# A gated recurrence and a maxout feed-forward on one core: 64x64 update tiles, a compact fp32 state, one PSUM ring and another written order

## The chip, the cores and the metric

The kernel runs on one core of a Trainium2 chip. TensorE (PE) multiplies matrices from SBUF into PSUM; VectorE (DVE), ScalarE (ACT) and GpSimd (POOL) work on elements, each an in-order queue with its own semaphores; SyncE (SP) issues nearly all DMAs, in order, to 16 DMA engines. [...] The metric is device time in microseconds (us) from the first to the last instruction and what lies around it; smaller is better.

## The reference, cut to what matters

```python
batch, n_heads, seq, head_dim = (4, 8, 768, 48)      # q, k, v, alpha: fp32
for t in range(S):
    state = alpha[:, :, t, :, None] * state + einsum('bhd,bhe->bhde', k[:, :, t], v[:, :, t])
    y[:, :, t] = einsum('bhd,bhde->bhe', q[:, :, t], state)
x = y.transpose(0, 2, 1, 3).reshape(B * S, H * D)    # 3072 x 384
h = maximum(maximum(x @ w1, x @ w2), x @ w3)         # w: 384 x 768
out = h @ w_out                                      # 768 x 384, fp32
```

Each of 8 heads keeps a 48 x 48 state that decays by alpha, row by row, and takes the outer product of k and v at every token.

## The kernel before, in words

**Steps.** The 3072 tokens are twelve steps of 256 tokens (`s`; batch `s % 4`, the part of the sequence `s // 4`). A step is two chunks of 128 tokens (`x` = 0, 1), which are worked on together: partitions 0 to 63 hold the first chunk, 64 to 127 the second, and each partition holds two neighbouring tokens (`r` = 0, 1). Steps s and s+4 belong to the same batch, so the state passes from chunk 0 to chunk 1 of a step, and from chunk 1 to chunk 0 of step s+4.

**One step, piece by piece.** Every piece has a letter, and the work's order is a written list of such letters. `l` loads alpha, k, q, v (384 KB each, `l0`, `l2` for q, and so on, L95), into rings of four. `m` multiplies the alphas of a token pair (L184), `N` takes the logarithm (L188), `r` makes 1/alpha (L193, L195), `u` and `w` shift k and q of the first token by it (L199, L203). `c` sums the logarithms on TensorE (L209, L212), `e`, `f`, `g` are the exponentials of the sums and totals on ScalarE (L217, L223, L229), `k` and `q` scale the inputs with them into fp16 (L235), `V` scales v (L156, L158). `T` turns scaled k and q with eight TensorE transposes a half (L259) and `t` copies them out of PSUM; from step 6 on `D` has a DMA do this instead (L267). `A` makes the scores (L280) and `a` masks them (L287). `Y` makes the output of both chunks (L311 from the state, L330 from the masked scores and v), `x` copies it to fp16 (`xT`).

**The state.** `S` makes the products of k and v of a chunk (L368). Two heads share 128 columns, so a product is 128 x 96 and only its two diagonal blocks of 48 are wanted. `s` adds the old state from the fp16 tile `st` into `full`, fp32 128 x 384 (L379). `M` makes the decay `gm` from the totals in two small operations (L353, L355); its second factor `half_c` is zero for the unwanted block of each partition. `z` multiplies `full` by `gm` into the other `st` (L383): this clears the unwanted blocks, and `Y` reads `st` directly.

**Feed-forward.** `G` makes one of nine gate products of a step (L396, six matmuls of 256 columns; three column blocks times w1, w2, w3). `h` copies the first of three on ScalarE (L150) and takes the maximum with the other two on VectorE (L411). `O` multiplies by w_out for one chunk (L420, six matmuls of 384 columns), `o` scales into `ob` and stores it (L428). `K` loads a weight block and `W` casts it. `H` issues matmuls on a tile of zeros that nobody reads (L433): fillers.

**Order.** There is no scheduler: each engine executes its instructions in the order in which the pieces are emitted. PROLOGUE is a free list for the first steps, STEADY is repeated for each step from the fourth on, and LAST ends it. A piece is a letter, an index, the engine if not the usual one (v VectorE, p GpSimd, a ScalarE), and the step after `@`. PSUM banks come from three rings, by a tag: `"w": 2, "s": 2, "g": 4` (work, state and output, gate). A piece that needs a bank takes one that is free at that place of the list, and its first matmul waits for whoever read the bank last.

**The output stage around the change.** Each chunk's output is three blocks of 128 columns (`f`) in one bank, made in four strips of 32 PSUM partitions (`m`). The state part goes in tiles of 128 rows by 32 columns, the chunk part in tiles of 64 by 32, and its order is

```python
        from_state(0, True)
        from_chunk((0, False), (1, True))
        from_state(1, False)
        from_state(2, True)
        from_chunk((2, False),)
```

Of the kernel before, what the change touches and what calls it, by code (L numbers as in the profile page):

```python
# [17 lines left out]
LAM = 0.09  # L18
# [5 lines left out]
def kernel(  # L24
# [43 lines left out]
    for u in range(U):  # L68
# [5 lines left out]
    undo = np.exp(-LAM * P)  # L74
    c32_np = np.stack(
        [np.exp(at_pair + SIGMA), np.exp(-at_token - SIGMA), undo * (rr < 64), undo * (rr >= 64)], 1
# [35 lines left out]
    c32 = cpool.tile([P, 4], FP32, name="c32")  # L112
# [5 lines left out]
    for item in """  # L118
        a0 c k0 q0 v0
    """.split():  # L120
        if item[0] == "c":
            load_const()
        elif item[0] == "w":
            load_weight(int(item[1:]))
        else:
            load(item[0], int(item[1:]))
# [3 lines left out]
    vs_c, ys_c, half_c = c32[:, 0:1], c32[:, 1:2], c32[:, 2:4]  # L130
# [29 lines left out]
    def cast_weight(_, i, eng):  # L160
# [8 lines left out]
     lps_of, dec_of, tps_of, aps_of, sps_of, gps_of, ops_of, full_of) = ({} for _ in range(19))  # L169

    banks = {"w": 2, "s": 2, "g": 4}

    def bank(shape, name, tag, dtype=FP32):
        return ps.tile(shape, dtype, name=name, tag=tag, bufs=banks[tag])
# [30 lines left out]
    def sums(s, _, tag):  # L205
        lps = bank([P, 512], "lps", tag or "w")
# [20 lines left out]
    def totals(s, *_):  # L227
        gate_of[s] = work.tile([P, HP, U, 2], FP32, name="ge", tag="ge", bufs=8)
        nc.scalar.activation(  # L229
            out=gate_of[s].rearrange("p a u b -> p (a u b)"),  # L230
            in_=lps_of[s][:, H * D:H * D + 2 * U * HP], func=AFT.Exp)
# [23 lines left out]
    def turn(s, r, tag):  # L255
        tps = bank([P, 2, HP, P], "tps", tag or "w", FP16)
# [14 lines left out]
    def scores(s, u, tag):  # L271
        aps = [bank([P, HP, P], f"aps{i}", tag or "w") for i in range(2)]
# [18 lines left out]
    def attend(s, _, tag):  # L291
# [3 lines left out]
        yps = [bank([P, NF, P], "yps", tag or "s") for _ in range(U)]  # L295
# [10 lines left out]
        def from_state(g, first):  # L306
            for x in range(U):
                for m in range(P // C) if old[x] else ():
# [4 lines left out]
                                     qkT[:, :, 0, p, x * J:(x + 1) * J], start=first, stop=not first)  # L313

        def from_chunk(*groups):
            jobs = []
            for m in range(P // C):
                todo = []
                for g, first in groups:
                    f = turns[m][g]  # L320
                    p, part = blocks[P // C * f + m]
                    cols = [(0, C * part)] * (part < 2) + [(1, D + C * (part - 1))] * (part > 0)
                    todo += [(f, first, n == 0, n == R * len(cols) - 1, i, p, n % R, at)
                             for n, (i, at) in enumerate(j for j in cols for _ in range(R))]
                jobs.append(todo)
            for n in range(max(len(j) for j in jobs)):
                for m, job in enumerate(jobs):
                    for x in range(U) if n < len(job) else ():
                        (f, first, begin, end, i, p, r, at), rows = job[n], slice(x * J, (x + 1) * J)
                        nc.tensor.matmul(  # L330
                            yps[x][C * m:C * (m + 1), f, :],
                            vt[rows, r * HP + p].rearrange("p a b -> p (a b)")[:, at:at + C],
                            lats[p // (HP // R)][rows, i, p % (HP // R) * R + r, :],
                            start=begin and (first or not old[x]),
                            stop=end and (not first or not old[x]))

        from_state(0, True)
        from_chunk((0, False), (1, True))
        from_state(1, False)
        from_state(2, True)  # L340
        from_chunk((2, False),)

# [197 lines left out]
```

## Time and profile before

| | us |
|---|---|
| median of 3 timed runs (159.69 to 161.0) | 160.05 |
| profiled execution, first to last instruction (its span; what lies around it is not in the page) | 157.2 |
| TensorE busy (2557 matmuls, 57 of them fillers) | 149.3 |
| VectorE busy (237 instructions) | 134.8 |
| ScalarE busy | 71.7 |
| GpSimd busy | 84.0 |
| gate products, 648 matmuls of mean 273 ns | 77.9 |
| output projections, 144 matmuls of mean 326 ns | 25.4 |

A matmul's duration in the page runs from its start to its modelled end, and matmuls are pipelined: gate products start 109 ns apart, and the 273 ns is not their price. Where the text counts TensorE's work, it takes the distance between starts. In the same way a VectorE instruction's row is about 0.08 us longer than the distance from its start to the next one's. Lists by group give `line engine operation output<-inputs sizes xcount | busy us, mean ns | idle time of the engine just before them <- what ended it`. Lists in order of time give start and length in us, with the idle time before a piece in brackets. The granted TensorE clock is full in all of the span, 0.9 or more in every fortieth.

### The profile page before, as it was taken

To read this page: it belongs to the slowest core of one execution; us is meant where nothing else is said; L and a number is where in the kernel's file an instruction comes from. 1 tells how busy PE (TensorE), PEld (TensorE's weight loads), DVE (VectorE), ACT (ScalarE), POOL (GpSimd) and SP (SyncE) were. 2 spreads that over 40 slices of the span, in tenths; PEclk is the share of its full clock that TensorE was granted. 3 is DMA by queue.
4 is the path that set the end of the run, shared out by engine and by line. 5 is a ranking of instruction groups with operands and counts; after the bars stand their busy time and mean duration, and the time that the engine had idled before them with its cause. 6 is when DMAs were issued, how large, how long until landed. Compare 5 with 4: busy or idle time off the path is not lost.

```text
span 157.2 us, 5971 instructions
## 1 busy us (share of the span) xinstructions
PE 149.3 (95%) x2557; PEld 111.0 (71%) x2557; DVE 134.8 (86%) x237; ACT 71.7 (46%) x146; POOL 84.0 (53%) x109
## 2 busy tenths in 40 slices
PE   6999986999999999999999999999999999999990
PEld 2346554888776796797787787877877877868850
DVE  2248999999977999999999999999999999696851
ACT  3348891776148466167165273371562621412020
POOL 5116679569325954946956928739759470100000
PEclk9999999999999999999999999999999999999999
DMA  5999999999999999369399999999709409120004
GB/s 123 321 325 325 355 355 249 329 368 261 235 291 276 301 280 321 111 168 286 68 173 274 223 252 263 136 265 202 203 5 103 134 4 203 35 80 24 4 34 167
DMA packets 70777, 31.97 MB, mean 203 GB/s; under 512 B 63328, under 2 KB 70752, under 8 KB 70752
## 3 DMA queue, kind: packets, MB, share of 16 engines
q1 hardware_dynamic: 70464, 31.46, 78.3%
q8 instruction: 20, 0.33, 0.8%
q10 hardware_dynamic: 288, 0.13, 0.6%
q14 instruction: 5, 0.04, 0.1%
HBM read 23.73 MB, written 4.72 MB: 181 GB/s over the span
## 4 chain that ended last, share of the span: by engine, by line
PE 88%; DVE 6%; ACT 2%; issue 1%
PE gps L396 44%; PE ops L420 15%; PE wps L433 9%; PE yps L330 6%; PE yps L311 4%; PE aps L280 4%; PE sps L368 3%; PE tps L259 2%; PE lps L209 1%; DVE vt L158 1%; DVE qk L235 1%; DVE hT L411 1%; DVE full L379 1%; ACT qkT L150 1%; PE lps L212 1%
## 5 line engine op out<-in xcount | busy, mean ns | idle before, releaser
L396 PE MATMUL gps<-xT,wcat 128*128 128x256 f16 x648 | 77.9, 273 | 2.3 <-DVE xT L152 2.3
L396 PEld LDWEIGHTS <-wcat 128*128 128x128 f16 x648 | 60.8, 98 | 12.4 <-ACT la L188 2.4
L287 DVE TENSOR_TENSOR lat<-aps,cp 128x512 f16<-128x512 f32 x48 | 30.5, 680 | 0.6 <-PE aps L280 0.6
L411 DVE TENSOR_TENSOR h<-gps,h 128x512 f16<-128x512 f32 x36 | 24.5, 685 | 3.1 <-PE gps L396 2.5
L411 DVE TENSOR_TENSOR hT<-gps,h 128x512 f16<-128x512 f32 x36 | 24.6, 687 | 2.4 <-PE gps L396 0.4
L420 PE MATMUL ops<-wo,hT 128*128 128x384 f16 x144 | 25.4, 326 | 0.1
L150 ACT CAST h<-gps 128x512 f16<-128x512 f32 x31 | 17.3, 584 | 13.6 <-PE gps L396 13.1
L383 POOL TENSOR_TENSOR st<-full,gm 128x384 f16<-128x384 f32 x11 | 9.3, 845 | 24.0 <-DVE full L379 20.0
L420 PEld LDWEIGHTS <-hT 128*128 128x128 f16 x144 | 14.0, 98 | 8.3 <-issue 0.3
L150 ACT CAST xT<-yps 128x384 f16<-128x384 f32 x12 | 5.8, 482 | 27.5 <-PE yps L330 27.5
L433 PE MATMUL wps<-blank 128*128 128x512 f16 x57 | 16.3, 438 | 1.2 <-DVE blank L505 1.2
L156 ACT ACTIVATE ob<-ops,c 128x384 f32<-128x384 f32 x13 | 7.3, 582 | 20.6 <-PE ops L420 20.6
L235 POOL TENSOR_TENSOR qk<-rq,ac 128x384 f16<-128x384 f32 x9 | 9.6, 1072 | 9.3 <-ACT ac L223 8.9
L203 POOL TENSOR_TENSOR qa<-rq,ra 128x384 f32<-128x384 f32 x10 | 10.0, 1001 | 4.6 <-DMA rq<-in_q_dram 4.6
L433 PEld LDWEIGHTS <-blank 128*128 128x128 f16 x57 | 6.0, 110 | 8.6 <-issue 3.7
L199 POOL TENSOR_TENSOR ka<-rk,ra 128x384 f32<-128x384 f32 x11 | 11.4, 1039 | 0.2 <-DMA rk<-in_k_dram 0.2
L235 POOL TENSOR_TENSOR qk<-rk,ic 128x384 f16<-128x384 f32 x8 | 10.2, 1274 | 1.6 <-ACT ic L217 1.6
L150 ACT COPY qkT<-tps 128x1024 f16<-128x1024 f16 x8 | 8.0, 1015 | 6.5 <-PE tps L259 6.5
L330 PE MATMUL yps<-lat,vt 64*32 64x128 f16 x768 | 10.9, 220 | 0.0
L158 DVE TENSOR_SCALAR ob<-ops,c 128x384 f32<-128x384 f32 x11 | 6.7, 608 | 3.1 <-PE ops L420 3.1
L379 DVE TENSOR_TENSOR full<-sps,st 128x384 f32<-128x384 f32 x16 | 8.8, 549 | 0.4 <-PE sps L368 0.3
L184 POOL TENSOR_TENSOR pa<-ra 128x384 f32<-128x384 f32 x9 | 9.0, 1002 | 0.0
(54 smaller groups left out, 186.7 us busy)
## 6 DMA issues: line engine op xcount, KB each, us to landing
ra<-in_alpha_dram SPq DMA_DIRECT2D x12, 384.0 KB, 4.8
rk<-in_k_dram SPq DMA_DIRECT2D x12, 384.0 KB, 5.0
rq<-in_q_dram SPq DMA_DIRECT2D x12, 384.0 KB, 5.4
rv<-in_v_dram SPq DMA_DIRECT2D x12, 384.0 KB, 5.4
out_dram<-ob SPq DMA_DIRECT2D x24, 192.0 KB, 3.5
ws<-in_moe_w_dram SPq DMA_DIRECT2D x9, 384.0 KB, 6.2
ws<-in_moe_w_out_dram SPq DMA_DIRECT2D x3, 384.0 KB, 7.6
qkT<-qk SPq DMA_TRANSPOSE x12, 4.7
```

What stands on the lines that cost most here:

```text
L150: nc.scalar.copy(out=dst, in_=src)
L199: engines[eng or "p"].tensor_mul(near_of[s, "k"], raw("k", s, 0), raw("a", s, 1))
L203: engines[eng or "p"].tensor_mul(near_of[s, "q"], raw("q", s, 0), inv1_of.pop(s))
L235: engines[eng or "p"].tensor_mul(dst.rearrange("p a b c -> p (a b) c")[:, :, :D], near_of.pop((s, n)) if r == 0 else raw(n, s, 1), dec_of[ ...
L287: nc.vector.tensor_mul(lat_of[s, u][:, i].rearrange("p (a r) t -> p a r t", r=R), aps_of[s, u][i].rearrange("p (a r) t -> p a r t", r=R), ...
L330: nc.tensor.matmul(yps[x][C * m:C * (m + 1), f, :], vt[rows, r * HP + p].rearrange("p a b -> p (a b)")[:, at:at + C], lats[p // (HP // R)] ...
L379: nc.vector.tensor_add(full, sps_of.pop((s, x)), sts[b][x].rearrange("p a (b d) -> p a b d", d=D))
L383: engines[eng or "p"].tensor_mul(sts[s % B][1 - x].rearrange("p a (b d) -> p a b d", d=D), full_of.pop((s, x)), gm_of.pop((s, x)).unsqueez ...
L396: nc.tensor.matmul(gps[:, j, :], wcat[:, f, g, jj * P:(jj + 1) * P], xT[:, f].rearrange("p u t -> p (u t)"), start=(f == 0), stop=(f == NF ...
L411: nc.vector.tensor_max(h, gps, h_of[s, i - 1])
L420: nc.tensor.matmul(ops, hT_of[s][:, jj, u * P:(u + 1) * P], wo16[:, jj, :], start=(jj == 0), stop=(jj == NJ - 1))
L433: nc.tensor.matmul(wps, blank[:, :P], blank, start=True, stop=True)
```

## The change

1. **Output stage.** All state products of a step's two chunks come first, then all chunk products, in one accumulation per bank.
2. **Update.** Each product is made in 64x64 tiles: one head's 64 (48 used) columns of k by its 48 columns of v. Only the wanted blocks are made, 320 matmuls of 48 columns for 160 of 96.
3. **State.** `full` is fp32 128 x 192. The decay `M` is one small multiplication; its constant factor moves into the bias of `g`. `z` writes `kept`, fp32 128 x 192, which the next `s` adds. A new piece `y` spreads `kept` into the fp16 `st` with zeros in the unwanted blocks, on GpSimd in one operation or on ScalarE in two.
4. **PSUM.** One ring of eight banks for all.
5. **Order.** One list for the whole run takes the place of PROLOGUE, STEADY and LAST. It begins with batches 1, 0, 3, 2; the constants are requested before the first load. Ten transposing pieces stay on TensorE (steps 0 to 4), and fourteen go by DMA (steps 5 to 11). The fillers go from 57 to 38. `V` is on ScalarE nine times (three before), `x` 16 (12), `o` 16 (13), `h` 34 (31), `y` 11. The last step's projections are in two parts each, four matmuls and two.

The core of the diff:

```diff
-        [np.exp(at_pair + SIGMA), np.exp(-at_token - SIGMA), undo * (rr < 64), undo * (rr >= 64)], 1
+        [np.exp(at_pair + SIGMA), np.exp(-at_token - SIGMA), rr < 64, rr >= 64, 0 * rr - LAM * P / 2], 1
...
-    banks = {"w": 2, "s": 2, "g": 4}
-    def bank(shape, name, tag, dtype=FP32):
-        return ps.tile(shape, dtype, name=name, tag=tag, bufs=banks[tag])
+    def bank(shape, name, dtype=FP32):
+        return ps.tile(shape, dtype, name=name, tag="bank", bufs=8)
...
-            in_=lps_of[s][:, H * D:H * D + 2 * U * HP], func=AFT.Exp)
+            in_=lps_of[s][:, H * D:H * D + 2 * U * HP], func=AFT.Exp, bias=undo_c)
...
+        for g in range(NF):
             for x in range(U):
                 for m in range(P // C) if old[x] else ():
                     f = turns[m][g]
                     p, part = blocks[P // C * f + m]
                     nc.tensor.matmul(yps[x][C * m:C * (m + 1), f, :],
                                      sts[b][x][:, p, C * part:C * (part + 1)],
+                                     qkT[:, :, 0, p, x * J:(x + 1) * J], start=(g == 0), stop=False)
...
+        for n in range(len(jobs[0])):
+            for m, job in enumerate(jobs):
+                for x in range(U):
+                    (f, begin, end, i, p, r, at), rows = job[n], slice(x * J, (x + 1) * J)
+                    nc.tensor.matmul(
+                        yps[x][C * m:C * (m + 1), f, :],
+                        vt[rows, r * HP + p].rearrange("p a b -> p (a b)")[:, at:at + C],
+                        lats[p // (HP // R)][rows, i, p % (HP // R) * R + r, :],
+                        start=begin and not old[x], stop=end and f == turns[m][-1])
...
-        gt = work.tile([P, HP], FP32, name="gt", tag="gt")
-        e.tensor_mul(gt, gate_of[s][:, :, x, 1], nxt)
-        gm = work.tile([P, HP, 2], FP32, name="gm", tag="gm", bufs=6)
-        e.tensor_mul(gm, gt.unsqueeze(2).broadcast_to([P, HP, 2]),
-                     half_c.unsqueeze(1).broadcast_to([P, HP, 2]))
+        gm = work.tile([P, HP], FP32, name="gm", tag="gm", bufs=6)
+        engines[eng or "p"].tensor_mul(gm, gate_of[s][:, :, x, 1], nxt)
...
                 for x in xs:
-                    rows = slice(x * J, (x + 1) * J)
-                    nc.tensor.matmul(sps_of[s, x][:, p],
-                                     qk[rows, r, 1, p].rearrange("p a b -> p (a b)"),
-                                     vt[rows, r * HP + p, :, :D], start=(r == 0), stop=(r == R - 1))
+                    for i in range(2):
+                        rows, cols = slice(x * J, (x + 1) * J), slice(64 * i, 64 * (i + 1))
+                        nc.tensor.matmul(sps_of[s, x][cols, p], qk[rows, r, 1, p, i],
+                                         vt[rows, r * HP + p, i, :D], start=(r == 0), stop=(r == R - 1))
...
-            nc.vector.tensor_add(full, sps_of.pop((s, x)),
-                                 sts[b][x].rearrange("p a (b d) -> p a b d", d=D))
+            nc.vector.tensor_add(full, sps_of.pop((s, x)), kept_of[b, U * c + x - 1])
...
+        kept = kept_of[b, U * c + x] = work.tile([P, HP, D], FP32, name="kept", tag="kept", bufs=6)
+        engines[eng or "p"].tensor_mul(kept, full_of.pop((s, x)),
+                                       gm_of.pop((s, x)).unsqueeze(2).broadcast_to([P, HP, D]))
+    def spread_state(s, x, eng):
+        c, b = divmod(s, B)
+        st, kept = sts[b][1 - x], kept_of[b, U * c + x]
+        if eng == "a":
+            for i in range(2):
+                nc.scalar.mul(st[:, :, D * i:D * (i + 1)], kept, half_c[:, i:i + 1])
+        else:
+            engines[eng or "p"].tensor_mul(
+                st.rearrange("p a (b d) -> p a b d", d=D), kept.unsqueeze(2).broadcast_to([P, HP, 2, D]),
+                half_c.unsqueeze(1).unsqueeze(3).broadcast_to([P, HP, 2, D]))
...
+    ORDER = """
+        l0@1 r0@1 m0v@1 N0@1 H12@0 c0@1 g0@1 f0@1 e0@1 l1@1 u0v@1 r1@1 l0@0 m0p@0 N0@0 l0@3
+        k1v@1 H10@0 c0@0 m0v@3 N0@3 H1@0 c0@3 e0@0 k0v@1 l2@1 q1v@1 l1@0 T1@1 l2@0 M0p@1 w0v@1
+        q0v@1 H1@0 T0@1 f0@0 q1p@0 r0@0 r1@0 u0v@0 t0a@1 k1v@0 l0@2 t1v@1 w0v@0 q0p@0 k0v@0 f0@3
+        g0@0 M0p@0 l3@1 g0@3 r0@2 r1@2 H5@0 A0@1 a1@1 l1@3 r0@3 a0@1 A1@1 T1@0 a3@1 H2@0 T0@0
+        t0v@0 m0p@2 V0a@1 H1@0 S0@1 u0p@3 a2@1 e0@3 k1v@3 t1a@0 k0v@3 H3@0 A0@0 s0a@1 z0p@1 N0@2
+        c0@2 a0@0 l2@3 r1@3 A1@0 a1@0 w0p@3 y0a@1 H1@0 Y0@1 l3@0 V0a@0 q0p@3 g0@2 f0@2 q1v@3
+        a2@0 S0@0 s0a@0 z0p@0 l2@2 w0p@2 q1v@2 T1@3 e0@2 l1@2 T0@3 a3@0 y0a@0 H2@0 Y0@0 x1a@1
+        x0a@1 K1@0 t0v@3 t1v@3 A0@3 A1@3 s1v@0 s1v@1 a1@3 W1a@0 k1p@2 G1@1 x0a@0 K0@0 W0a@0
...
+        q1p@9 g0@9 l3@9 h6a@7 h1v@7 A1@8 a2@8 S0@8 s0v@8 A0@8 a0@8 V0v@9 k1p@9 D1@9 k0p@9 q0p@9
+        G5@7 D0@9 r1@10 a3@8 c0@10 f0@10 g0@10 M1v@6 N0@11 l2@11 y1a@4 a1@8 O1@5 o1a@5 O0@5
+        o0a@5 h5v@7 G7@7 h7v@7 z0p@8 y0p@8 e0@10 k1p@10 u0p@10 c0@11 e0@11 h2v@7 Y0@8 f0@11
+        g0@11 x0v@8 S0@9 A1@9 A0@9 x1a@8 G6@8 M0v@9 a2@9 a1@9 l2@10 l3@10 M1p@5 z1p@5 k0p@10
+        l1@11 G3@8 h3a@8 G4@8 s0v@9 z0p@9 a0@9 y0a@9 G8@8 G7@8 h8v@7 h6a@8 M1p@7 G0@8 G5@8 a3@9
+        h7v@8 w0v@10 G1@8 h4v@8 z1p@7 y1p@5 Y0@9 q1v@10 x0v@9 M0p@10 z1v@6 x1a@9 D1@10 q0v@10
...
+        x0v@11 O0@6 o0v@6 G8@11 G0@11 h1v@10 h0a@11 O1@6 o1a@6 G6@11 G4@11 G1@11 h8v@10 h4v@10
+        h5v@10 h1v@11 h2v@10 G2@11 G7@11 G3@11 G5@11 h3a@11 h4v@11 O1@8 O0@8 o1v@8 h5v@11 o0a@8
+        O1@9 h2v@11 h6a@11 h7v@11 h8v@11 O0@9 o0v@9 o1a@9 O0@10 o0a@10 O2@11 O3@11 o0a@11 O4@11
+        O5@11 o1v@11 O1@10 o1a@10
+    """
```

## The prediction, made blind

> **What bounds the kernel now.** I read the engines' busy times first, then the chain that ended last, the busy times by stage, and TensorE in order of time. From the page, the busy times and the chain by engine:
>
> ```profile
> PE 149.3 (95%) x2557; PEld 111.0 (71%) x2557; DVE 134.8 (86%) x237; ACT 71.7 (46%) x146; POOL 84.0 (53%) x109
> ...
> PE 88%; DVE 6%; ACT 2%; issue 1%
> ```
>
> The same by stage (us from the span's start; after the stretch's length the busy us of each engine, then clock, DMA share, GB/s):
>
> ```profile
> 0.00:25.00 25.00, 21.32 (x274) 11.16 (x274) 16.40 (x32) 15.58 (x30) 12.73 (x20) 1.00 1.05 302
> 25.00:64.00 39.00, 38.65 (x665) 30.43 (x666) 35.92 (x62) 21.64 (x42) 24.39 (x33) 1.00 1.01 287
> 64.00:128.00 64.00, 64.00 (x1231) 50.08 (x1229) 62.18 (x113) 29.05 (x64) 43.99 (x54) 1.00 0.82 173
> ```
>
> After 25 us TensorE is never short of work, and from 64 to 128 us VectorE is busy 97% beside it. Before 25 us most of TensorE's work is filler, as its order of time shows (start, us, instruction):
>
> ```profile
> 9.61 0.33 PE L209 MATMUL lps<-la,cp 128*128 128x384 f16 x1
> 9.77 0.24 PE L212 MATMUL lps<-cp,la 128*128 128x4 f16 x4
> 9.87 3.61 PE L433 MATMUL wps<-blank 128*128 128x512 f16 x16
> ...
> 22.17 0.64 PE L280 MATMUL aps<-qkT 48*64 48x128 f16 x32
> 25.08 0.82 PE L396 MATMUL gps<-xT,wcat 128*128 128x256 f16 x6 [2.27 <-DVE xT L152]
> ```
>
> So the span splits, by start-to-start times of the trace, into 1.2 us to the first matmul, 15.8 of fillers (57), 2.5 idle before the first gate product at 25.08, 133.6 of useful matmuls, and 4.1 from the last matmul's start to the end: 157.2. The time is this span plus what lies around it. The median of the runs, 160.05, is 2.85 above the span; I keep that difference. Two things can move the end: the useful matmuls' sum, and how much of it is done when the dense part begins.
>
> **The useful sum.** One output stage L311/L330 in the steady part:
>
> ```profile
> 98.34 0.30 PE L311 MATMUL yps<-qkT,st 128*32 128x128 f16 x8
> 98.56 0.60 PE L330 MATMUL yps<-lat,vt 64*32 64x128 f16 x48
> 99.10 0.41 PE L311 MATMUL yps<-qkT,st 128*32 128x128 f16 x16
> 99.43 0.30 PE L330 MATMUL yps<-lat,vt 64*32 64x128 f16 x16
> 99.67 1.48 PE L396 MATMUL gps<-xT,wcat 128*128 128x256 f16 x12
> ```
>
> The starts tell the cost of a change of tile shape. Within a run, matmuls start 7.6 ns (chunk) or 11.4 ns (state) apart on average; state to chunk takes 149 ns, chunk to state 153. The change puts all state products first, so one crossing of each kind goes per step: 12 x 0.30 = **3.6 us**. Steps 0 to 4 alone are turned on TensorE, not 0 to 5: 16 transposes x 57 ns = **0.9**. Two shape changes fewer in the rest of the order, some 0.13 each: 0.3.
>
> The update (L368) goes from 160 matmuls of 64 rows and 96 columns, a pair of which takes 42.5 ns, to 320 of 48 columns in 64x64 tiles, four to a round and as many rounds as before (96: eight a step, with a single matmul for a pair in the last four steps). The trace has no such form. The nearest is the scores (L280), whose rounds of four tiles of 128 columns take 56 ns. Scaled to 48 columns that is 22 ns, which would save 96 x 20 ns = 1.9 us; with the full 56 ns it costs 96 x 13.5 ns = 1.3 us. I take zero, since the pair's own row lies between. [...]
>
> Useful work: 133.6 - 3.6 - 0.9 - 0.3 = **128.8 us**.
>
> **VectorE, ScalarE, GpSimd.** The groups that the compact state touches (busy, mean ns of one, idle before):
>
> ```profile
> L379 DVE TENSOR_TENSOR full<-sps,st 128x384 f32<-128x384 f32 x16 | 8.8, 549 | 0.4 <-PE sps L368 0.3
> L383 POOL TENSOR_TENSOR st<-full,gm 128x384 f16<-128x384 f32 x11 | 9.3, 845 | 24.0 <-DVE full L379 20.0 <-ACT full L150 1.6 <-ACT ra L195 1.3
> L383 DVE TENSOR_TENSOR st<-full,gm 128x384 f16<-128x384 f32 x9 | 5.4, 597 | 0.0
> L353 DVE TENSOR_TENSOR gt<-ge 128x4 f32<-128x4 f32 x9 | 3.8, 422 | 0.0
> ```
>
> On VectorE consecutive starts are 0.60 us apart for 512 elements, 0.47 for 384 and 0.14 for 4; 192 elements come to 0.30 by a straight line. By these spacings, counting every piece of both orders, VectorE falls from 119.9 to **108.5 us**: state and gates go from 14.5 to 6.5 us; six of nine scalings of v, three of 77 operations on gate products, four of twelve copies of the output, three of eleven scalings before a store and one weight cast leave it; ten more products of the inputs and two more transposed copies come to it. ScalarE takes it up, 65 to 77 us of 150, and GpSimd goes from 77 to 73. This costs nothing by itself; it gives back the cover that VectorE lacks now. The added spreading of the state is bounded on ScalarE by twice its 16-element and its 384-element row (0.19 and 0.52), so 0.4 to 1.0 us; I take 0.5, for two halves of 192. On GpSimd it is 0.83, the row of L383. It lengthens the path sum, decay, spread, output by 0.2 to 1 us. Counted in TensorE's own work, the new order leaves 3 to 10 us between update and output, which hides it, but only 1.4 and 2.0 in steps 0 and 1, which lie inside the start below.
>
> **The start.** DMA sets the pace: SP issues a load every 1.19 us and it lands about 4.8 later, so load number n (from 4) lands near 4.6 + 1.19(n-1), and the first three at 4.6, 5.9 and 7.2. In the new order decay input 1 lands at 4.6, and 12 cold fillers of 427 ns end at 6.3, so the first decay sums start at 6.3 (9.6 now). VectorE then works nearly without rest. Up to the last transposed copy ahead of the first gate product it has 8 masks and 4 copies x 0.60 and 16 products x 0.47, 14.7 us. It waits some 1.5 us (exponential 1.0, third decay input 0.3, q 0.2), and GpSimd beside it stretches operations as it does now (products of 0.55 that take 0.8 to 1.3), 3 us. That ends at 4.6 + 14.7 + 1.5 + 3 = 23.8, and with step 3's scores the first gate product starts at **24.5**. Its weight block, load 15, lands at 21.3 and is cast by 22.2, so VectorE sets it, not DMA. The next blocks (loads 16, 17, 19 to 21) land at 22.5 to 28.5, ahead of their places.
>
> By then TensorE has done steps 1 and 0 whole and step 3 up to its scores: 8.7 us of useful work, against 6.2 at 25.08 now.
>
> **Sum.** 24.5 + (128.8 - 8.7) + 4.1 = 148.7 us without a stall. I add 2.8 for stalls that the old order doesn't have. Steps 8 and 9 have 4.6 us of TensorE work between the second DMA transpose and the first score, where the old order has 6.4 or more. The row is
>
> ```profile
> qkT<-qk SPq DMA_TRANSPOSE x12, 4.7
> ```
>
> (4.7 us to landing, 5.5 at most), plus 1.3 of the second one's issue: 1.4 short in each if SP gets there only then, half of it taken, 1.4. The way from output to next gate product needs 1.1 and has 1.1 to 1.2, so 0.1 in each of nine steps, 0.9. The second half's spread state in step 9 is emitted right ahead of its reader: 0.5. Span 151.5, **time 154.4 us**.
>
> **Rivals.**
> - *No stalls, and the update at its lower bound*: 148.7 - 1.9 + 2.85 = 149.7. For it: the old order stalls for 0.7 us in all after 25. Chance 0.17.
> - *VectorE stays the bound to about 60 us.* When TensorE's sum is 40.6 (the fillers left out), VectorE's is 41.7. If contention stretches it by 15% and not the 10% of now, the gates wait for their maxima some 3 to 4 us more: 158. Chance 0.12; up to 160, no change, 0.08.
> - *Late loads and transposes in SP's one queue: slower.* The old loop emits a load 14 to 36 us of TensorE work ahead of its use, the new order mostly 0 to 15, and seven steps, not six, come through the transposing DMA. Each transpose waits for its products, and every load and store behind it with it. If each of the seven steps loses over 1.5 us, that is 10.5, and 148.7 + 10.5 + 2.85 = 162 is slower than now. At 2 us a step it is 166. Against it: DMA's share is only 0.3 to 0.7 between 112 and 136 us now, and SP, not following TensorE's order, can run ahead. Chance 0.13.
> - *The clock*: only 38 fillers, 16 of them in the 14 us before the first gate product. Now an idle stretch of 2.5 us keeps the clock at 9 tenths and over in every slice. [...] The trace's own bound is the cold filler's 427 against 216 ns, so 2 us for some 10 such: inside the main case.
>
> **Chances.** Main case (152 to 157) 0.50. Faster by over 1%: 0.50 + 0.17 + 0.12 = 0.79; within 1% 0.08; slower 0.13. (1% is about what a measurement of this kernel can tell from no change.) The range runs from 149.7, the stall-free case, to 161.5, where the slower rival begins.
>
> **What would show it.** First decay sums near 6.3 and first gate product near 24.5; each output stage with one crossing; VectorE clearly below 97% from 64 to 128; after 25 us TensorE idle under 3 us, at scores that wait for qkT. It is wrong if TensorE waits for transposes step after step, if gate products wait for maxima up to 60 us, or if the 64x64 updates take over 0.5 us each.

## The result and the profile after

The changed kernel takes 155.76 us (median of 4 runs, 155.34 to 157.8) beside 160.16 for the kernel before on the same chip: a ratio of 0.972, interval 0.967 to 0.976. The forecast was 154.4. The profiled execution has a span of 154.3 us (157.2 before) and a time of 156.12, 1.8 more than its span.

First the page of the changed kernel: span, busy times, the granted clock in 40 slices, the instruction queue and the chain by engine.

```profile
span 154.3 us, 6211 instructions
...
PE 142.9 (93%) x2682; PEld 108.8 (70%) x2682; DVE 118.1 (77%) x214; ACT 87.4 (57%) x182; POOL 79.0 (51%) x105
...
PEclk9999999999999959999999999999999999999998
...
q8 instruction: 21, 0.34, 0.8%
...
PE 76%; SPq 11%; DMA 4%; issue 4%; ACT 2%; DVE 1%; DVEq 0%; ACTq 0%
```

VectorE has lost 16.7 us of busy time and ScalarE gained 15.7, as intended. Two things are new: "issue", time in which TensorE waited for nothing that the profile shows, stands for 4% of the chain (1% before), and one slice of the clock, 54 to 58 us, is at 5 tenths. The same by stage (columns as in the prediction):

```profile
0.00:25.00 25.00, 21.27 (x418) 11.88 (x418) 17.40 (x37) 17.57 (x38) 14.74 (x23) 1.00 1.02 280
25.00:64.00 39.00, 36.57 (x697) 30.18 (x686) 30.54 (x53) 26.84 (x53) 25.21 (x32) 0.96 1.07 282
64.00:128.00 64.00, 62.31 (x1292) 49.88 (x1291) 54.81 (x100) 34.18 (x77) 38.52 (x51) 1.00 0.89 192
```

From 64 to 128 us VectorE falls from 97% to 86%, so it is no longer close to being the bound. TensorE, however, is now idle for 2.4 us between 25 and 64, and for 1.7 in the next stretch, where it had been idle for 0.35 and 0. The view of waits, over the whole span, says what it waited for, with one line of ScalarE (us in all, times, longest):

```profile
PE yps L316 <- issue: 2.9, 2, 2.1
...
ACT wcat L141 <- DMA ws<-in_moe_w_dram: 1.8, 2, 1.3
...
PE aps L269 <- issue: 1.0, 1, 1.0
...
PE gps L380 <- issue: 0.5, 1, 0.5
```

No DMA transpose and no VectorE result is in these TensorE lines. TensorE in order of time, at the longest of those stalls:

```profile
49.00 0.35 PE L300 MATMUL yps<-qkT,st 128*32 128x128 f16 x12
49.28 0.74 PE L316 MATMUL yps<-lat,vt 64*32 64x128 f16 x64
49.95 0.52 PE L300 MATMUL yps<-qkT,st 128*32 128x128 f16 x24
50.40 0.47 PE L316 MATMUL yps<-lat,vt 64*32 64x128 f16 x33
53.00 0.41 PE L316 MATMUL yps<-lat,vt 64*32 64x128 f16 x31 [2.13 <-issue]
53.34 7.74 PE L380 MATMUL gps<-xT,wcat 128*128 128x256 f16 x54
60.92 0.33 PE L198 MATMUL lps<-la,cp 128*128 128x384 f16 x1
```

Two output stages stand back to back. In the middle of the second, after its 33rd chunk matmul, TensorE stops for 2.3 us, and the view of waits names no operand and no bank for it. Then 54 gate products take 7.6 us from start to start, much of it at the lower clock; with the clock up they take 5.9 (the fence of shift32 below).

**What stops it.** Each matmul comes with a weight load, so 2682 of each and some others make 5379 TensorE instructions. The instruction queue moved 0.34 MB in 21 pieces, 16 KB each. Counting TensorE's instructions in the trace, every stall of over 0.6 us that the profile gives to "issue" falls on an instruction whose number, counted from 0, leaves 193 on division by 256. Between two such places lie 256 instructions, as many as a fetched piece holds (5379 / 21), so they are read here as the edges of the pieces, called blocks below. Own count from the trace; all columns but the first two in us, and "in the block" is the time TensorE needed from entering the block before to running into its end:

```
after     instr.  stops at  goes on  stall   in the block   fetch of next block
           705     23.12     24.12    1.00       3.6           21.69 - 22.63
          1985     50.65     52.99    2.34       1.6           50.72 - 51.72
          3265     88.22     88.94    0.72       4.5           86.70 - 87.63
          4033    106.25    107.51    1.26       1.8          105.22 - 106.16
before   shortest 256 instructions after 25 us: 4.46 us; no stall at any block's end
```

Each fetch takes 0.93 to 1.00 us in these rows (0.9 to 1.5 in all of this profile and of the one before), and TensorE goes on 1.3 to 1.5 us after its end. This holds in all fourteen profiles of this case: no fetched block begins less than 1.2 us after the end of its fetch, and at the 33 edges with a stall of 0.25 us or more TensorE goes on 1.2 to 1.6 us after it. A block that is used up before then shows as a stall. The back-to-back outputs use up a block in 1.6 us, and output 8, update 9 and scores 9 near 105 us in 1.8. In the old order no 256 instructions after 25 us run in under 4.46 us.

The start, TensorE first and ScalarE's cast of the first gate weights below it:

```profile
6.28 0.42 PE L198 MATMUL lps<-la,cp 128*128 128x384 f16 x1
...
24.55 0.64 PE L269 MATMUL aps<-qkT 48*64 48x128 f16 x32
25.48 0.83 PE L380 MATMUL gps<-xT,wcat 128*128 128x256 f16 x6 [0.29 <-ACT wcat L141]
```

```profile
24.59 0.83 ACT L141 CAST wcat<-ws 128x768 f16<-128x768 f32 x1 [1.33 <-DMA ws<-in_moe_w_dram]
```

The decay sums start at 6.28, as forecast (6.3). The first gate product starts at 25.48, not 24.5, and its last wait is for a weight block: issued by SP at 18.03, landed at 24.5, not 21.3. VectorE had done its early work by 23.0.

One output stage of the steady part, to set beside the five lines shown for before:

```profile
83.12 0.52 PE L300 MATMUL yps<-qkT,st 128*32 128x128 f16 x24
83.56 0.74 PE L316 MATMUL yps<-lat,vt 64*32 64x128 f16 x64
84.23 1.15 PE L406 MATMUL ops<-wo,hT 128*128 128x384 f16 x6
```

From its first start to the next stage's it takes 1.11 us; before, it was 99.67 - 98.34 = 1.33. So it saves 0.22 us a step, not 0.30. The groups of the compact state (busy, mean ns of one, idle before):

```profile
L354 DVE TENSOR_TENSOR full<-sps,kept 128x192 f32<-128x192 f32 x16 | 5.5, 349 | 0.4 <-PE sps L344 0.4
L344 PE MATMUL sps<-vt,qk 64*64 64x48 f16 x320 | 5.2, 188 | 0.3 <-ACT vt L147 0.2
...
L359 POOL TENSOR_TENSOR kept<-full,gm 128x192 f32<-128x192 f32 x18 | 9.8, 545 | 18.8 <-DVE full L354 16.2
...
L367 ACT ACTIVATE st<-kept,c 128x192 f16<-128x192 f32 x22 | 8.8, 448 | 2.6 <-POOL kept L359 2.5
```

### The profile page after: what moved, and what is told of

It is laid out like the page before. It is cut to its first block, busy times and chain, and to the rows that moved or that the text cites. A ratio compares the mean times of both kernels' runs of the same rounds, so it can differ in the third digit from the quotient of the medians.

```text
span 154.3 us, 6211 instructions
## 1 busy us (share of the span) xinstructions
PE 142.9 (93%) x2682; PEld 108.8 (70%) x2682; DVE 118.1 (77%) x214; ACT 87.4 (57%) x182; POOL 79.0 (51%) x105
## 4 chain that ended last, share of the span: by engine, by line
PE 76%; SPq 11%; DMA 4%; issue 4%; ACT 2%; DVE 1%; DVEq 0%; ACTq 0%
PE gps L380 48%; PE ops L406 14%; SPq L94 11%; PE yps L316 5%; DMA ws<-in_moe_w_dram 4%; PE aps L269 3%; PE yps L300 3%; PE sps L344 2%; PE tps L248 1%; PE lps L198 1%; ACT wcat L141 1%; DVE h L397 0%; DVE hT L397 0%; PE lps L201 0%; ACT h L141 0%
## 5 line engine op out<-in xcount | busy, mean ns | idle before, releaser
L141 ACT CAST h<-gps 128x512 f16<-128x512 f32 x34 | 19.9, 585 | 21.6 <-PE gps L380 14.5
L359 POOL TENSOR_TENSOR kept<-full,gm 128x192 f32<-128x192 f32 x18 | 9.8, 545 | 18.8 <-DVE full L354 16.2
L406 PEld LDWEIGHTS <-hT 128*128 128x128 f16 x144 | 13.5, 98 | 8.1
L419 PE MATMUL wps<-blank 128*128 128x512 f16 x38 | 12.4, 459 | 1.2 <-DVE blank L492 1.2
L224 POOL TENSOR_TENSOR qk<-rq,ac 128x384 f16<-128x384 f32 x7 | 7.0, 1001 | 12.0 <-ACT ac L212 8.5
L316 PEld LDWEIGHTS <-vt 64*32 64x32 f16 x768 | 7.3, 90 | 4.6 <-issue 3.3
L367 ACT ACTIVATE st<-kept,c 128x192 f16<-128x192 f32 x22 | 8.8, 448 | 2.6 <-POOL kept L359 2.5
L182 ACT ACTIVATE ra<-ra 128x384 f32<-128x384 f32 x12 | 6.3, 526 | 6.5 <-DMA ra<-in_alpha_dram 6.5
L269 PE MATMUL aps<-qkT 48*64 48x128 f16 x384 | 8.8, 219 | 1.1 <-issue 1.0
L188 POOL TENSOR_TENSOR ka<-rk,ra 128x384 f32<-128x384 f32 x8 | 8.4, 1047 | 2.5 <-DMA rk<-in_k_dram 2.5
L269 PEld LDWEIGHTS <-qkT 48*64 48x64 f16 x384 | 6.3, 106 | 3.3 <-issue 2.0
```

Of the source, the lines that this page charges most:

```text
L141: nc.scalar.copy(out=dst, in_=src)
L224: engines[eng or "p"].tensor_mul(dst.rearrange("p a b c -> p (a b) c")[:, :, :D], near_of.pop((s, n)) if r == 0 else raw(n, s, 1), dec_of[ ...
L269: nc.tensor.matmul(aps[i][cols, a * R + r, :], qkT[rows, r, 1, p, cols], qkT[rows, :, 0, p, cols], start=True, stop=True)
L316: nc.tensor.matmul(yps[x][C * m:C * (m + 1), f, :], vt[rows, r * HP + p].rearrange("p a b -> p (a b)")[:, at:at + C], lats[p // (HP // R)] ...
L359: engines[eng or "p"].tensor_mul(kept, full_of.pop((s, x)), gm_of.pop((s, x)).unsqueeze(2).broadcast_to([P, HP, D]))
L406: nc.tensor.matmul(ops, hT_of[s][:, jj, u * P:(u + 1) * P], wo16[:, jj, :], start=(jj == 0), stop=(jj == NJ - 1))
```

## The experiments

The theories when they began: (A) the stalls and the fallen clock come from instruction fetch, so they follow the instruction count and not the work; (B) they belong to the place in the work (a bank, an operand, the change of tile shape). Later runs ask what the parts of the change are worth alone, and whether the losses can be taken out. Each ratio is to the kernel before, run on the same chip.

**Moving the instruction count, not the work.** The first block of fillers, 12 matmuls of 512 columns whose result nobody reads, is cut into more and narrower ones with nearly the same columns in all. Every later instruction moves on by 8, by 160, and by 32.

```diff
+        n, width = (16, 384) if n == 12 else (n, 512)      # shift8
+        n, width = (92, 64) if n == 12 else (n, 512)       # shift160
+        n, width = (28, 220) if n == 12 else (n, 512)      # shift32
...
-            nc.tensor.matmul(wps, blank[:, :P], blank, start=True, stop=True)
+            nc.tensor.matmul(wps[:, :width], blank[:, :P], blank[:, :width], start=True, stop=True)
```

> The first filler piece, 12 matmuls of 512 columns, becomes 16 of 384: the same columns and the same time, 8 TensorE instructions more ahead of everything else. Theory of code fetch: TensorE's stalls without a releaser come at every 256th instruction, where the next 16 KB of code hasn't landed, and each stretch of 256 that is worked off in under some 4.5 us stalls. Then the stalls stay at the same remainder of the instruction count, 4 matmuls earlier in the work, and the stretches that end near 50 and 106 us, now 3.97 and 3.05 us long with their stalls, hold still denser work: stalls 3 to 5 us longer in sum, 158 to 161 us. Rival, a wait on data or on a PSUM bank at those places: the stalls stay at the same matmuls with the same length, 155.8 us.

Measured: 154.39 us, 0.971 (0.963 to 0.980). The stalls are at instructions 705, 1985, 3265 and 4033 again, and so 4 matmuls earlier in the work: 1.97 us at 24.25, 0.88 at 53.97, 0.25 at 88.12, 0.49 at 105.90. The place follows the count; that is (A). Their sizes don't repeat, and my time was too high by several us: I had taken the sizes for fixed by the place. The clock falls here after the first stall (1.97 us), not at 54.

> The same piece becomes 92 matmuls of 64 columns (5888 columns for 6144): 160 TensorE instructions more ahead of everything else. Code fetch: the boundaries now fall so that no stretch of 256 instructions after 25 us is shorter than 4.4 us; the stalls at 50.7, 88.2 and 106.3 us (2.1, 0.5 and 1.1 us) go, and with the longest of them the fall of the clock behind it (54 gate products in 7.7 us for 5.9, 1.8 us): 155.8 - 3.7 - 1.8 = 150.3, between 150 and 152.5. Rival, a wait on data or on a bank: 155.8 as before the shift, stalls in place.

Measured: 155.66 us, 0.981 (0.973 to 0.988). The stalls near 50, 88 and 106 us are gone, as (A) says, but new ones stand at instructions 705 (20.97 us, 0.68 long), 961 (25.05, 2.52) and 2241 (56.71, 0.55). The clock falls at 27.3. TensorE in order of time around the longest:

```profile
24.19 0.73 PE L316 MATMUL yps<-lat,vt 64*32 64x128 f16 x64
24.86 0.41 PE L269 MATMUL aps<-qkT 48*64 48x128 f16 x13
27.57 0.75 PE L269 MATMUL aps<-qkT 48*64 48x128 f16 x19 [2.31 <-issue]
28.25 1.04 PE L380 MATMUL gps<-xT,wcat 128*128 128x256 f16 x4
```

That block was entered at 21.64, its next one's fetch began only at 25.09, and TensorE went on at 27.57: 5.9 us for a block, where the change needed 3.05 with its stall near 105 us. It delays the first gate product to 28.25. I had counted on a fixed time for a block, and missed by 5 us. That the early blocks come late because DMA is then full (in the change a share of 1.02 in the first 25 us, 0.89 from 64 to 128) fits, but no run here isolates it.

> The changed kernel with only the first filler piece cut into 28 matmuls of 220 columns (32 TensorE instructions more ahead). Code fetch: the block that ended in the stall near 50 us now begins inside the two output stages' run and holds fewer of their instructions, so the stall shrinks from 1.5 to 2.3 us to under 1.5, the one at 104 to 106 us from 1.3 to 1.8 to under 0.5, and the one at 88 us goes; 1.5 to 3 us less than the changed kernel. All stalls at remainder 193 of 256. Data waits: no change.

Measured: 152.55 us, 0.959 (0.952 to 0.965). Sixteen more matmuls that nobody reads make the kernel 2 to 3 us faster than the change as given (0.972 and, below, 0.980); its first gate product is at 25.11, so the start gives at most 0.4 of it. Two stalls remain, 0.77 at 22.88 and 1.08 at 51.74. The same two output stages as above:

```profile
51.17 0.52 PE L300 MATMUL yps<-qkT,st 128*32 128x128 f16 x24
51.62 0.34 PE L316 MATMUL yps<-lat,vt 64*32 64x128 f16 x17
52.82 0.59 PE L316 MATMUL yps<-lat,vt 64*32 64x128 f16 x47 [0.86 <-issue]
53.35 6.07 PE L380 MATMUL gps<-xT,wcat 128*128 128x256 f16 x54
59.25 0.33 PE L198 MATMUL lps<-la,cp 128*128 128x384 f16 x1
```

The edge is now 16 matmuls earlier, the stall is half as long, and the 54 gate products start 5.9 us before the next stage. (The clock falls in this run too, but at 25.2.) That is the row from which the fallen clock's price is taken: 60.92 - 53.34 = 7.58 against 59.25 - 53.35 = 5.90, **1.7 us**.

**The change again, as it stands.**

> The changed kernel once more, beside the next three on one chip. Expected 0.965 to 0.976 of the kernel before. Code fetch: the stalls stand at the same instructions as in its first profile (every one at remainder 193 of 256), with lengths that differ by up to 1 us; a wait on data or a bank would not keep to that remainder.

Measured: 155.94 us, 0.980 (0.970 to 0.991). Stalls at 51.00 (1.45) and 103.57 (1.81), at instructions 1985 and 4033, and 0.35 at 29.4; the clock is at 7 tenths in two slices after the second. The first gate product is at 24.96. So the places are fixed for a kernel, and the size of each stall varies from one execution to the next by a microsecond.

**One part alone in the old kernel, one part undone in the new.** The state products first, put into the kernel before, and the old order of the output put back into the changed one.

```diff
-        from_state(0, True)
-        from_chunk((0, False), (1, True))
-        from_state(1, False)
-        from_state(2, True)
-        from_chunk((2, False),)
+        for g in range(NF):      # all state products, start=(g == 0), stop=False
+            ...
+        for n in range(len(jobs[0])):      # then all chunk products
+            ...
```

> The kernel before with the new output stage alone (all state products, then all chunk products), its order and all else as it was. TensorE alone the bound: two crossings of 149 and 153 ns less in each of twelve steps, 3.6 us, so 156.5. VectorE as second bound (97% busy from 64 to 128 us): TensorE's gain turns into waits for gate maxima and masks, and less than half of it shows, 158.5 to 160.

Measured: 158.26 us, 0.996 (0.992 to 1.000). By the starts of the trace the output stages take 13.5 us in place of 15.35, 1.85 less, and the 13.5 hold a wait for VectorE of about 0.4. But the span is only 0.4 us shorter. The stretch from 25 to 64 us of this kernel:

```profile
25.00:64.00 39.00, 37.29 (x658) 29.88 (x659) 35.77 (x62) 20.94 (x41) 24.00 (x32) 1.00 1.01 289
```

TensorE falls from 38.65 to 37.29 busy us, so it is idle for 1.4 us more, while VectorE stays at 35.8 of 39. Most of what TensorE saves it waits out, since VectorE is nearly as full: the view of waits names VectorE's masked scores, state sums and copies of the output (`xT`). So in the old kernel the part alone is worth next to nothing. That the relief of VectorE is what it lacks is argued from these waits, not shown.

> The changed kernel with the old output stage (state and chunk products by turns), all else as changed. TensorE the bound with VectorE loose (86% from 64 to 128 us): all 3.6 us come back, 159.4. If the crossings were hidden behind other waits now, less than 1.5 of it: under 157.3. The number of instructions is the same, so code boundaries stay; a stretch that is spread by the crossings (4 x 0.15 us about two outputs) shortens the stall at 50 us by up to 0.6.

Measured: 156.47 us, 0.974 (0.966 to 0.982). Its output stages (without the fetch stalls in them) take 16.8 us against 14.1 in the change: the **2.7 us** that the part is worth in TensorE time. The whole time can't tell this from the change (0.972 and 0.980): the runs of this kernel alone lie between 154.3 and 158.2 us. Its profile also stalls on "issue", 2.29 us at 52.4 and 0.81 at 108.1, at instructions 1985 and 4033 once more, and its clock falls after the first.

**The parts without the new order.** The old order and loops, with the update, the compact state, the gates and the output of the change. The spreading of the state, which the old order lacks, had to be put somewhere: in the first version on GpSimd ahead of the loop and on ScalarE in it, ahead of an exponential.

```diff
-        ... z1v@-2 h0@0 q1p@2 S0@1 e0@2
+        ... z1v@-2 h0@0 y1a@-2 q1p@2 S0@1 e0@2
```

> The kernel before with all parts of the change but the order and the one PSUM ring: output stage with state first, 64x64 update, compact state with its spreading (placed behind each decay in the prologue on GpSimd; on ScalarE in the repeated part). TensorE-bound with VectorE relieved: useful work falls by 3.0 (output, as measured by undoing it) and 1.9 (update), and the 2.6 us of new waits between 30 and 45 us of the kernel with the output stage alone fall to about 1: 4 us less than before, ratio 0.975, the same as the changed kernel; then the order as such brought nothing. If the new order carries the gain, the ratio stays above 0.985. Code fetch: 160 more update matmuls, but spread over steps; no stall over 0.6 us after 26 us.

Measured: 170.57 us, 1.069 (1.059 to 1.079). From 67 us on, the scores of every step lose 1.24 us, seven times in all, and two early outputs lost 3.4 and 2.2 waiting for GpSimd's spread state. TensorE, and then ScalarE, at one of these places:

```profile
102.42 0.44 PE L279 MATMUL aps<-qkT 48*64 48x128 f16 x17
103.88 0.41 PE L279 MATMUL aps<-qkT 48*64 48x128 f16 x15 [1.02 <-ACT ic L216]
```

```profile
102.65 0.80 ACT L377 ACTIVATE st<-kept,c 128x192 f16<-128x192 f32 x2 [0.64 <-DVE kept L369]
103.36 0.47 ACT L216 ACTIVATE ic<-lps 128x384 f32<-128x384 f32 x1
```

The two halves of the spreading wait for VectorE, with the exponential (L216) queued behind them. The exponential's end releases the bank of the decay sums, which the scores want next. The clock falls twice as well, at 43.2 and 60.3 us, after the waits of the two outputs. So this run prices my placing, not the parts: one wait put ahead of the release of a bank cost 7 x 1.24 = 8.7 us, twice what the whole change brings.

In the second version the spreading comes right before its reader, or behind the exponential, and all banks come from one ring of eight.

```diff
-        return ps.tile(shape, dtype, name=name, tag=tag, bufs=banks[tag])
+        return ps.tile(shape, dtype, name=name, tag="bank", bufs=8)
...
-        ... z1v@-2 h0@0 y1a@-2 q1p@2 S0@1 e0@2
+        ... z1v@-2 h0@0 q1p@2 S0@1 e0@2 y1a@-2
```

> As old_order_new_parts, but with the one ring of eight PSUM banks, and every spreading on ScalarE: right ahead of its reader in the prologue, behind the exponential e of the next step in the repeated part. In the earlier run the second scores of each step waited 1.24 us for ScalarE's reading of the decay sums' bank, behind which the spreading stood. If the placing and the bank were all that was wrong, the period of the repeated part falls from 11.5 to 10.2 us and the whole to 0.97 to 0.985 of the kernel before. If the old order has no room for the spreading on any engine, it stays above 1.0, and the new order is what makes room for it.

Measured: 158.30 us, 0.988 (0.982 to 0.993). From 64 to 128 us:

```profile
64.00:128.00 64.00, 62.99 (x1309) 50.06 (x1307) 61.96 (x109) 39.32 (x92) 41.06 (x49) 1.00 0.79 173
```

VectorE is still busy for 61.96 of 64 us: it is the order that hands its work to ScalarE, not the smaller state. Placed like this, the parts bring about 1.2%; the rest of the change's 2.0 to 2.8% comes with the new order. The 1.2% still holds 3.1 us of outputs waiting for ScalarE's spread state (four times) and a fall of the clock at 23.7; what the parts would bring if they were placed better in the old order isn't shown.

**Can the losses be taken out?** First the back-to-back outputs are separated: output 3 goes ahead of other products, and its copies with it.

```diff
-        G8@1 h8v@1 M0p@4 ... G6@2 h6a@2 G7@0 h7v@0 ...
-        Y0@3 h8v@0 ... x1a@3 x0a@3 h7v@2
+        G8@1 h8v@1 Y0@3 M0p@4 ... G6@2 h6a@2 x1a@3 x0a@3 G7@0 h7v@0 ...
+        h8v@0 ... h7v@2
```

> The output stage of step 3 is moved some 2.6 us ahead, to behind the gate piece G8 of step 1, and its copies with it, so that it no longer stands next to the output stage of step 4; the same instructions in all. Code fetch: the block of 256 instructions that ended in the 2.1 us stall near 50 us now holds 48 gate instructions (2.6 us) more and output instructions fewer: the stall falls to under 0.6 us, the clock stays full from 53 to 62 us, 1.6 + 1.8 us less than the changed kernel. The early stall (23 us) and those at 88 and 106 us stay. Rival (the stall comes from data for step 4's output): it stays, no gain.

Measured: 154.47 us, 0.968 (0.959 to 0.977). The block that ends at instruction 1985 now holds 4.0 us of work and not 1.6; the stall there is 1.22 us in this profile, where I had expected under 0.6, and the one at 4033 is 0.98. No slice of the clock falls. The intervals of this kernel and of the change overlap.

Next, the first two weight blocks are loaded earlier in SP's queue, to bring the first gate product forward.

```diff
+        ... z0p@0 K1@0 l2@2 w0p@2 q1v@2 T1@3 e0@2 K0@0 l1@2 ...
-        x0a@1 K1@0 t0v@3 ... x0a@0 K0@0 W0a@0
+        x0a@1 t0v@3 ... x0a@0 W0a@0
```

> The changed kernel with the first two weight blocks loaded one and two loads earlier, nothing else. Weight load as what sets the first gate product: it starts up to 1 us earlier than 25.0 to 25.5, and the whole takes up to 1 us less. Code fetch beside it: the first gate product stays at 25 or later, and the whole within 0.5 us of the changed kernel.

Measured: 156.12 us, 0.976 (0.969 to 0.984): no gain. Step 0's output, which comes before the first gate product, stalls for 1.52 us at instruction 705, and the first gate product is at 26.54. The weight is in time and the fetch isn't. The later stalls are 2.14 at 51.97, 0.59 at 89.2 and 0.62 at 107.0.

The early weights, the separated outputs and the 28 narrow fillers together:

> The same, and the first two weight blocks are loaded one and two loads earlier, and the first filler piece is cut into 28 matmuls of 220 columns for 12 of 512 (32 TensorE instructions more). If the first weight block set the start (its cast waited 1.3 us for the load), the first gate product comes 0.3 to 1 us earlier than 25.5; if the code fetch near 23 us set it, it stays at 25.2 to 25.5. Code fetch also says: the stalls at 88 and 106 us shrink to under 0.4 us in sum. Together 3.5 to 5 us less than the changed kernel: 150 to 152 us where that has 155. Data waits: no more than 1 us less.

Measured: 151.68 us, 0.954 (0.946 to 0.963). ScalarE near the first gate product, and TensorE's last wait before it:

```profile
22.99 0.84 ACT L141 CAST wcat<-ws 128x768 f16<-128x768 f32 x1
25.28 0.48 ACT L141 CAST xT<-yps 128x384 f16<-128x384 f32 x1 [1.46 <-PE yps L316]
```

```profile
22.76 0.30 PE L316 MATMUL yps<-lat,vt 64*32 64x128 f16 x13
24.61 0.62 PE L316 MATMUL yps<-lat,vt 64*32 64x128 f16 x51 [1.55 <-issue]
```

The cast starts at 22.99 without a wait for DMA. What remains is the fetch stall (1.77 us from start to start), and 0.87 at 51.02. The clock is at 9 tenths in all 40 slices.

> split_early_shift once more, with more rounds: 0.945 to 0.96 of the kernel before, with no fall of the clock and, after 26 us, code stalls of under 1.5 us in sum.

Measured: 153.18 us, 0.957 (0.951 to 0.963). This profile stalls for 2.02 us at 23.57, and for 0.70 to 0.88 at 74, 87 and 93, and its clock falls at 25.2; I had expected no fall, and under 1.5 us of stalls after 26. The two sets of runs agree on 4 to 5% against the kernel before, where the change as given has 2 to 3. The 32 more instructions alone (0.959) do nearly all of that; separating the outputs or loading the weights earlier adds nothing that these intervals resolve.

## Why the prediction was right and where not

The sign, the mechanism and the size held: VectorE ceased to crowd TensorE, less TensorE work remained, and the dense part began with more of it done. The time is 1.4 us above the forecast. Its terms, however, were off by more than that and partly cancelled, so that it came so near is in part luck (us, spans):

```
forecast span                                             151.5
the start: first gate product 25.5, not 24.5               +1.0
the update: at its lower bound, not at zero                -1.9
the output: 0.22 a step, not 0.30                          +1.0
the 2.8 of stalls that I added (transposes and others)     -2.8
fetch stalls after the first gate product                  +4.1
the lower clock from 54 to 58                              +1.7
not accounted for                                          -0.3
measured span                                             154.3
```

- **The start.** "First decay sums at 6.3" held (6.28), and VectorE's end of early work came at 23.0 (23.8). The step "VectorE sets it, not DMA" failed: the weight block took 6.5 us from issue to landing where I had put 4.8 for all loads, and was issued 1.5 us later than the straight line says. With the block early, the fetch stall takes over (split_early_shift), so the true order of lateness is DMA, fetch, VectorE.
- **The useful sum.** The mis-sized term is the crossing of the output. I took both changes of shape, 149 and 153 ns, for pure cost. But the last round of a run has its own 53 to 57 ns in that interval, which stays when the crossing goes. By the stage rows 12 x 0.22 = 2.6 us were saved, not 3.6; the 2.7 of after_oldout agrees, and the 1.85 of before_statefirst, with its wait of 0.4, nearly.
- **The update.** I took zero between -1.9 and +1.3. By start-to-start times, 160 matmuls took 5.5 us and 320 take 3.65, so the lower end was right. Part of it I hadn't seen at all: update and scores now have the same 64x64 tile, and passing between them takes 46 ns at most, mostly under 20, where 132 to 148 were paid. Within a run the 64x64 matmuls start 9.3 ns apart on average; in the run at 42.1 us a round of four takes 32 ns, where the two scalings gave 22 and 56.
- **The stalls.** This is the step that failed in kind. I added 1.4 us for DMA transposes, 0.9 from output to gate and 0.5 for a spreading. The view of DMA issues of the changed kernel has (median us to landing last)

```profile
qkT<-qk SPq DMA_TRANSPOSE x14, 4.1
```

  where I had 4.7, and no score waited for a DMA transpose (the one wait of 0.5 us for a `qkT`, at 12.8, was for ScalarE's copy of a TensorE transpose). The stalls that came instead are instruction fetch, which I hadn't named even as a rival. Its traces stood in the page of before: a queue of instructions with 20 pieces and 0.33 MB, and output stages of 88 matmuls and as many weight loads in 1.33 us.
- **Spreading the state.** Two halves on ScalarE take 0.8 us together (bounds 0.4 to 1.0, taken 0.5). The new order hid them after the first gate product; ahead of it, TensorE's weight loads for the outputs of steps 1 and 0 waited 0.2 to 0.6 us for them, four times. In the old order the same spreading, badly placed, made the kernel 7% slower.
- **Rivals.** VectorE as the bound to 60 us is excluded by its row (30.54 of 39). Its busy time fell by 16.7 us, more than the 11.4 that the prediction summed from spacings; where the rest comes from wasn't taken apart. Late loads in SP's queue cost the first gate product 1 us, and not one microsecond in each step. The stall-free case, 149.7, wasn't reached by any run; the best of them, at 151.68, still has 2.6 us of fetch stalls. The clock, "inside the main case" at 2 us, did fall and cost 1.7, but after a stall and in the middle, not before the first gate product.
- **What lies around the span.** I added 2.85, a median less one profiled span. The time of the changed kernel's profiled execution is 1.8 above its own span. The rest was scatter between executions. The median after is only 1.46 above the profiled span, so 1.4 of the 2.8 us by which my span was too short didn't show in the time.

## What to carry to other kernels

Where TensorE runs many small tiled matmuls, count instructions as well as time: look for the shortest stretch of 256 instructions (matmuls and weight loads together, what one 16 KB piece held here). In this case every block used up in under 3 us had an "issue" stall that no wait explains, and so had some of 3.2 to 5.6. Two things were tried against it: keeping two such bursts apart (split_y, 0.968, not told from the change's 0.972 and 0.980), and a few unread matmuls early in the program that move the block edges (shift32, 0.959). A crossing between tile shapes should be priced by whole stages before and after, not by the gap between two starts. And the difference between time and span is to be taken from the same execution.

## What the runs showed that was not expected

**Instruction fetch can stop TensorE.** Issue stalls of over 0.6 us fell on one position in 256, lasted up to 2.5 us, moved with the count of instructions (shift8, shift160, shift32) and came where a block was used up in 1.6 to 5.6 us. The next block began 1.2 to 1.6 us after its fetch had ended. In the kernel before no edge shows a stall; here the stalls take 4.1 us of 154.3 after the first gate product. What decides when a fetch starts stays open: it lies between 1.7 us before and 4.1 us after the entry into the block ahead of it. It is later while DMA is fuller (2.1 us after on average for blocks entered before 60 us, 0.5 for those after 100, all profiles together), but no run took that apart.

**The clock fell by windows, not by the length of a stall.** Stalls of 1.97 us and more after 23 us were followed by lower clock in the change, shift8, shift160, early_w, after_oldout and split_again; 1.77 us in split_early_shift wasn't, 1.81 in the second profile of the change was, and so was a mere 0.77 in shift32. The kernel before was idle for 2.49 us and kept its clock. What parts these cases can be read from the traces, though no run was made to test it. In each execution the stretches of clock that the profile records begin and end on one grid of 3.41 us (in the change, the falls at 54.26 and 153.25 are 29 steps apart), and its place differs from run to run. I counted the work of every such window from the first record on: a matmul's columns, at the 216 ns of a 512-column filler, times its tile's part of 128 x 128, the largest tile in the trace. The eleven windows with a fall behind them, in all fourteen profiles, hold 0.17 to 0.33 of a full window; all others hold 0.35 or more (the windows in which the work ends left aside). The idle 2.49 us of before and the 1.77 of split_early_shift are cut in two by an edge of the grid, at 23.95 and 23.70, while the 0.77 of shift32 stands in a window that is mostly small tiles (0.31). So, by these counts, where a stall falls on the grid and what stands around it count, and the first changes from run to run.

The recorded clock is 0.5 for one window after each of the eleven, which costs half of 3.41 us, the 1.7 measured above. The records begin only at 6.9 us in the kernel before; its fillers start 427 ns apart until 6.7 and 216 after, so the full clock of the page doesn't hold for all of its span. None of the eleven windows was idle: each held at least 0.17 of its full work.
